# Softmax exponentials per unit on ScalarE with bias and summed output, and sinks in float32, in an attention and mixture-of-experts kernel

## The chip, the cores and the metric

The kernel runs on one core of a Trainium2 chip. The metric is the device time of one execution in microseconds (us). The kernel before has a median of 838.93 us over three runs (838.45 to 840.20). Engines: PE is the matmul engine (TensorE), PEld its weight load, DVE is VectorE, ACT is ScalarE, POOL is GpSimd, SP the engine whose queue issues most DMAs.

## The reference, cut to what matters

```python
# q, k, v: (4, 8, 768, 64) float32; n_sink 4; window 128
scores = (q @ k.transpose(0, 1, 3, 2)) / np.sqrt(64)
keep = (key < 4) | ((query - key >= 0) & (query - key < 128))
scores = np.where(keep, scores, -1e9)
a = np.exp(scores - scores.max(-1, keepdims=True))
a = a / (a.sum(-1, keepdims=True) + 1e-9)
x = (a @ v).transpose(0, 2, 1, 3).reshape(3072, 512)
noisy = x @ w_gate + np.log1p(np.exp(x @ w_noise)) * noise      # (3072, 8)
# two largest experts of each row; their softmax, with 1e-9 in the divisor, as weights
out = sum over these two of weight * (np.maximum(x[rows] @ w1[e], 0) @ w2[e])
```

## The kernel before, in words

**Phase one** (0 to 228 us) is the attention and the choice of experts. It has 48 steps n: 16 pairs of heads g (four batches of four pairs), and for each three blocks jj of 256 queries. A step holds four *units* u: two query tiles of 128, two heads. A query tile looks at two key tiles of 128: after masks, each query has 128 keys of the window, kept at columns modulo 128, and four sinks, so a unit is 128 queries by 132 scores (KW), and a step's tile in `cbuf` is 128 x 528, plus one extra column for each unit that holds 1e-9.

A step goes through these functions. `turn` (PE, L280) transposes two key and two query tiles; `turn_c` (ACT, L286) copies all 512 columns out of PSUM into `kq`; `ksink` (POOL, L290) puts the sinks' keys beside them. `qk` (PE, L307) makes the scores S; `prev` (ACT, L310) copies sinks and the earlier key tile into `cbuf`, `cur` (DVE, L315 or L317) puts the masked current tile over it. `mins` (DVE, L327) takes each unit's maximum, `sub` (POOL, helper `minus` at L192) subtracts it from the 528 columns, `exps` (ACT, L334) exponentiates all four units in one instruction with the scale 1/8, `sums` (DVE, L337) adds up each unit with its 1e-9 column, `sums_i` (DVE, L345) inverts the sums. `ptr` (PE, L365) transposes the window's probabilities into P, `ptr_c` (ACT, L368) copies them to CT, `ptr_m` (POOL, L377, or DVE, L375) makes the masked copy CM. The sinks' probabilities are split in a high and a low part in the PE's reduced 32-bit type (fp32r), by `pcopy` (ACT, L356, or POOL, L354) and `plow` (POOL, L192). `pv` (PE) first transposes them (L382), then multiplies CT by v (L388) and CM by the difference dv of neighbouring value tiles (L391; `dv` is on POOL for one pair in four, else on DVE). `sink_c` (ACT, L395) copies the transposed sinks' probabilities to `ps`, `sinks` (PE, L400) multiplies them by the sinks' values `vr` and adds this into the same PSUM tile X. `pv_c` (ACT, L408), `rows` (PE, L413), `rows_c` (DVE, L416, into `xr`) and a DMA to `x_rows` end the step.

The sinks' values of a batch reach `vr` by a memset on POOL (L241), 16 DMAs on SP's queue (L247), a rounding on ACT (`sink_hi`, L251) and the rest on DVE (`sink_lo`, L256). The choice of experts for a finished batch (lines 546 to 870: projections at L590, operations on 48 columns such as L676 on DVE, spreading of row numbers by four matmuls at L808) is mixed in with the next batches. So are loads of the experts' weights through `st`, whose low parts POOL subtracts (`w<-st,w`, at L192). At the end of phase one gathered rows are transposed (T, L883) and their low part `sqn` made on DVE.

**Phase two** (228 to 837 us) runs the eight experts: H (L999 to L1001), Y (L1028 to L1030), the weighted copy of Y on ACT with a per-row scale (L1037), and a scatter to `out` (L1052).

The order of the work is made by `Plan`, a list scheduler in Python that runs while the program is written: each operation has an engine, a cost, a priority (its step plus an offset from the table `PR`; `_0` for the first two pairs, `_9` for the last two) and the operations that it depends on. On each engine the program has the operations in the order of their planned start. For PE, an operation of another *kind* (shape of stationary tile) than the one before is put back. Rings of buffers bound how far engines run apart: five tiles of `cbuf`, three maxima, four sums, three `pcbuf`, two S, two X, one P and one T in PSUM.

Of the kernel before, what the change touches and what calls it, by code (L numbers as in the profile page):

```python
# [20 lines left out]
PR = dict(dv_pool=1, cm_pool=11, gap=1.5, pc_pool=4, warm=1, cur=11.119, cur1=0.687, cur1_0=44.511, cur1_9=-33.328,  # L21
          cur_0=298.594, cur_9=103.16, dv=-0.483, dv_0=16.276, dv_9=183.829, exps=904.17, exps_0=41.004, exps_9=-4.57,
          ga=1192.414, gt=-84.555, ksink=-94.534, ksink_9=51.556, lg=-15.298, load_qk=-1.606, load_v=-787.643,
          mins=168.634, mins_0=-734.152, mins_9=-446.873, nosink=-377.158, nosink_0=-548.293, nosink_9=-11.556,
          pcopy=43.317, pcopy_0=835.726, pcopy_9=1.286, plow=31.263, plow_0=22.235, plow_9=9.949, prev=-44.255,
          prev_0=3.084, prev_9=-520.412, ptr=290.156, ptr_0=2279.933, ptr_9=-183.508, ptr_c=121.858, ptr_c_0=-0.024,
          ptr_c_9=-10.11, ptr_m=217.241, ptr_m_0=-0.246, ptr_m_9=-22.839, pv=-903.99, pv_0=-10.446, pv_9=-0.801,
          pv_c=2.756, pv_c_0=123.068, pv_c_9=40.062, qk=55.827, qk_0=107.566, qk_9=-45.834, rows=41.788, rows_0=71.983,
          rows_9=-173.605, rows_c=-520.43, rows_c_0=-0.232, rows_c_9=0.725, rt=-379.032, sink_c=-1407.554,
          sink_c_0=45.426, sink_c_9=-0.086, sinks=-132.305, sinks_0=-79.407, sinks_9=-258.405, sub=443.589, sub_0=-14.389,  # L30
          sub_9=-3.573, sums=98.341, sums_0=-6.429, sums_9=-5.607, sums_i=29.922, sums_i_0=-62.833, sums_i_9=-0.83,
          t0=294.759, t2=376.526, tgroup=-1.35, tgroup_0=-158.265, tgroup_9=240.162, tgroup_c=-950.066, tgroup_c_0=76.182,
          tgroup_c_9=-18.757, w1=-543.239, ksink_0=-147.432, stay=3020.27)
# [161 lines left out]
def attention(tc, plan, consts, cst, sh, q, k, v, xbuf):  # L195
# [20 lines left out]
    cbuf = consts.tile([128, plan.rings["C"], 4, KW + 1], F32, name="cbuf")  # L216
    nc.gpsimd.memset(cbuf[:, :, :, KW:], 1e-9)

    pcbuf = consts.tile([128, plan.rings["pc"], 128], F32R, name="pcbuf")
    nc.gpsimd.memset(pcbuf.bitcast(F32), 0.0)  # L220
    bit = [consts.tile([128, 1], dt, name=nm) for nm, dt in (("biti", I32), ("bit", F32))]
    nc.gpsimd.iota(bit[0], pattern=[[0, 1]], base=0, channel_multiplier=1)
    nc.vector.tensor_scalar(bit[0], bit[0], 3, 1, op0=OP.logical_shift_right, op1=OP.bitwise_and)
    nc.vector.tensor_scalar(bit[1], bit[0], -1.0, None, op0=OP.mult)
    bit = bit[1]
    vst = [plan.next("st") for _ in range(sh.B)]
# [16 lines left out]
    def sink_values(b):  # L243
        for u in range(4):
            for x in range(4):
                r = 4 * NS * u + NS * x
                nc.sync.dma_start(vs(b)[r:r + NS, u // 2, :, u % 2, :],  # L247
                                  dram(v, (b * HP * 2 + u % 2) * S * D, [[D, NS], [2 * S * D, HP], [1, D]]))

    def sink_hi(b):  # L250
        nc.scalar.activation(get("vr", b, [128, 2, HP, 2, D], F32R), vs(b), AF.Copy)  # L251

    def sink_lo(b):

        t = get("vr", b)
        nc.vector.scalar_tensor_tensor(t, t.bitcast(F32), bit, vs(b), op0=OP.mult, op1=OP.add)  # L256
# [1048 lines left out]
```

## Time and profile before

| what | before |
|---|---|
| median of three runs | 838.93 us (838.45 to 840.20) |
| the profiled execution's own time | 838.36 us |
| its span, first to last instruction | 836.8 us |
| PE busy | 801.9 us (96%) |
| PEld busy | 682.0 us (82%) |
| DVE busy | 442.0 us (53%) |
| ACT busy | 345.6 us (41%) |
| POOL busy | 437.0 us (52%) |

The profile is one execution with every instruction's start and length. Busy times count instructions in flight; matmuls are pipelined and overlap, so what a matmul costs is read from start to start. The granted clock (PEclk) is a share of PE's full speed. A wait is the idle time of an engine just before an instruction, put down to what released it.

### The profile page before, as it was taken

The page shows a single profiled execution, that of the slowest core. Times are in us where ns is not written, and L with a number is a line of the kernel's source. Part 1 is how long each engine was busy: PE and PEld are TensorE (multiplying, and loading weights), DVE is VectorE, ACT ScalarE, POOL GpSimd, SP SyncE. Part 2 cuts the span into 40 slices and gives each one's busy share as a digit, 9 for nine tenths or more (in the row PEclk, how much of TensorE's full clock was granted, in tenths as well). Part 3 has the DMA queues.
Part 4 walks back from the last instruction along what each step waited for, and adds up shares of the span by engine and source line. Part 5 has one row for each costly group of instructions (what it writes and reads, how often), then busy time and mean ns, then how long its engine had stood idle before and what let it go on. Part 6 is the DMA issues. An engine that isn't in the chain of part 4 may idle for free.

```text
span 836.8 us, 13639 instructions
## 1 busy us (share of the span) xinstructions
PE 801.9 (96%) x4901; PEld 682.0 (82%) x4901; DVE 442.0 (53%) x1098; ACT 345.6 (41%) x685; POOL 437.0 (52%) x602
## 2 busy tenths in 40 slices
PE   6999998998899999999999999999999999999995
PEld 3776776776689989888988988898898889889984
DVE  5788979897573444155345435534543553454210
ACT  4787776775422243234233333413333341333211
POOL 5565866877416742263652746365274636617303
PEclk9999999999999999999999999999999999999998
DMA  6749877754544665165355626535462643544113
GB/s 119 152 90 235 183 184 175 177 137 114 163 115 110 167 149 133 16 160 127 69 100 130 118 40 162 126 68 100 129 118 40 162 126 66 104 119 68 26 23 45
DMA packets 151814, 97.23 MB, mean 116 GB/s; under 512 B 100704, under 2 KB 129376, under 8 KB 151744
## 3 DMA queue, kind: packets, MB, share of 16 engines
q1 hardware_dynamic: 137744, 67.93, 31.6%
q0 software_dynamic: 14000, 28.40, 19.7%
q8 instruction: 39, 0.64, 0.3%
q14 instruction: 31, 0.25, 0.1%
HBM read 67.44 MB, written 28.85 MB: 115 GB/s over the span
## 4 chain that ended last, share of the span: by engine, by line
PE 77%; DVE 8%; issue 5%; POOL 4%; DMA 3%; ACT 2%; SPq 0%; another core or an unknown queue 0%; DVEq 0%; POOLq 0%; ACTq 0%
PE H L999 11%; PE H L1000 11%; PE H L1001 11%; PE Y L1030 10%; PE Y L1028 10%; PE Y L1029 10%; PE S L307 3%; PE X L388 2%; PE T L280 2%; PE P L365 1%; PE Y L1034 1%; PE Y L1033 1%; POOL out L1052 1%; DMA x_rows<-xr 1%; PE X L391 1%
## 5 line engine op out<-in xcount | busy, mean ns | idle before, releaser
L1052 POOL DMA_INDIRECT out<-y,idx x56 | 93.0, 1660 | 238.6 <-ACT y L1037 228.8
L840 POOL DMA_INDIRECT xg<-x_rows,rt_idq x182 | 183.4, 1008 | 55.5 <-issue 51.8
L1017 DVE SCALAR_TENSOR_TENSOR h<-H,h 128x384 fp32r<-128x384 f32 (+1 forms) x192 | 80.8, 445 | 224.7 <-ACT h L1010 224.7
L999 PE MATMUL H<-skn,w 128*128 128x384 f32 (+2 forms) x544 | 187.5, 345 | 0.0
L1010 ACT ACTIVATE h<-H 128x384 fp32r<-128x384 f32 (+2 forms) x136 | 68.0, 500 | 288.0 <-PE H L1001 287.9
L1000 PE MATMUL H<-sqn,w 128*128 128x384 f32 (+2 forms) x544 | 186.7, 343 | 0.0
L1001 PE MATMUL H<-skn,w 128*128 128x384 f32 (+2 forms) x544 | 186.0, 342 | 0.0
L999 PEld LDWEIGHTS H<-skn,w 128*128 128x128 f32 x544 | 102.5, 188 | 8.8 <-issue 0.8
L1000 PEld LDWEIGHTS H<-sqn,w 128*128 128x128 f32 x544 | 102.5, 188 | 7.5
L1001 PEld LDWEIGHTS H<-skn,w 128*128 128x128 f32 x544 | 102.5, 188 | 3.9
L1028 PE MATMUL Y<-w2b,h 128*128 128x512 f32 x196 | 76.8, 392 | 0.9 <-ACT h L1010 0.9
L1030 PE MATMUL Y<-w2b,h 128*128 128x512 f32 x196 | 77.1, 393 | 0.6 <-DVE h L1017 0.6
L1028 PE MATMUL Y<-w2a,h 128*128 128x512 f32 x196 | 77.5, 395 | 0.0
L1029 PE MATMUL Y<-w2a,h 128*128 128x512 f32 x196 | 76.9, 392 | 0.0
L1030 PE MATMUL Y<-w2a,h 128*128 128x512 f32 x196 | 76.9, 392 | 0.0
L1029 PE MATMUL Y<-w2b,h 128*128 128x512 f32 x196 | 76.8, 392 | 0.0
L192 POOL TENSOR_TENSOR cbuf<-cbuf,mn 128x528 f32<-128x528 f32 x48 | 52.1, 1087 | 25.4 <-DVE mn L327 20.2
L307 PE MATMUL S<-kq 64*128 64x264 f32 (+1 forms) x384 | 56.6, 406 | 3.8 <-DVE cbuf L317 2.6
L897 ACT ACTIVATE skn<-xtn 128x512 fp32r<-128x512 f32 (+1 forms) x49 | 28.9, 598 | 58.8 <-DVE xtn L888 58.8
L1030 PEld LDWEIGHTS Y<-w2b,h 128*128 128x128 f32 x196 | 36.8, 188 | 9.1 <-DVE h L1017 1.0
L307 PEld LDWEIGHTS S<-kq 64*128 64x128 f32 x384 | 31.8, 192 | 14.7 <-issue 4.8
L1030 PEld LDWEIGHTS Y<-w2a,h 128*128 128x128 f32 x196 | 36.8, 188 | 8.4
(193 smaller groups left out, 1361.6 us busy)
## 6 DMA issues: line engine op xcount, KB each, us to landing
st<-in_moe_w SPq DMA_DIRECT2D x36, 512.0 KB
st<-in_moe_w SPq DMA_DIRECT2D x112, 128.0 KB
out<-zt SPq DMA_DIRECT2D x31, 256.0 KB
vn<-in_v SPq DMA_DIRECT2D x16, 384.0 KB
x_rows<-xr SPq DMA_DIRECT2D x48, 128.0 KB
kn<-in_k SPq DMA_DIRECT2D x30, 192.0 KB
qn<-in_q SPq DMA_DIRECT2D x30, 192.0 KB
xg<-x_rows,rt_idq POOLq DMA_INDIRECT x182, 2.9
```

The costliest lines, as they stand in the source:

```text
L192: eng.tensor_tensor(out, a, b, op=OP.subtract)
L307: nc.tensor.matmul(p[:, :2 if j else 1], kq(g)[r, j // 2, 2 + j % 2, NS:], x[:, :2 if j else 1], start=True, stop=True)
L840: nc.gpsimd.indirect_dma_start(out=x[:, i, :], out_offset=None, in_=xbuf.rearrange("r (q d) -> (r q) d", d=sh.SW), in_offset=bass.Indirect ...
L999: nc.tensor.matmul(p, w[:, 0, i], xh, start=(i == 0), stop=False)
L1000: nc.tensor.matmul(p, w[:, 0, i], xl, start=False, stop=False)
L1001: nc.tensor.matmul(p, w[:, 1, i], xh, start=False, stop=(i == DC - 1))
L1010: nc.scalar.activation(get("h", FC * q + f, [128, 896], F32R)[:, :width], get("H", FC * q + f), AF.Relu)
L1017: nc.vector.scalar_tensor_tensor(h[:, o:o + s1 - s0], p[:, s0:s1], 0.0, h[:, s0:s1].bitcast(F32), op0=OP.max, op1=OP.subtract)
L1028: nc.tensor.matmul(p, hh, w[:, 0], start=(f == 0), stop=False)
L1029: nc.tensor.matmul(p, hh, w[:, 1], start=False, stop=False)
L1030: nc.tensor.matmul(p, hl, w[:, 0], start=False, stop=(f == FC - 1))
L1052: d = nc.gpsimd.indirect_dma_start(out=out, out_offset=bass.IndirectOffsetOnAxis(ap=c["idx"][:size(e, t), e, t:t + 1], axis=0), in_=get("y ...
```

## The change

- The mask constants change sign, and the scores with them: `turn_c` becomes `turn_k` (ACT, 256 columns of keys, L270) and `turn_q` (DVE, 256 columns of queries, times -1/8, L275). `mins` takes the minimum.
- `sub` is gone. `exp_sum` (ACT, L322) does one unit of 132 columns at a time, with scale -1, the unit's minimum as bias and the unit's sum as second output. `sums` is gone; `sums_a` adds 1e-9 to four sums (30 steps on DVE, L325, and 18 on POOL). The extra columns of `cbuf` go.
- The sinks' probabilities stay float32: `plow` is gone, `pcopy` has 16 columns (36 steps on ACT, L343, 12 on POOL, L341), and their transposition is an operation of its own, `pctr` (L346), ahead of `pv`. `vr` is float32 and filled by four DMAs a batch (L239); both roundings go. The product with the sinks' values (L385) is a float32 matmul.
- `dv` is on POOL for three pairs in four, and the masked copy CM on DVE for 16 of 48 steps (four before).
- All offsets in `PR` are others, and `sinks` has no kind of its own any more.

The numbers of `PR` are left out of the diff.

```diff
+    def turn_k(g, gi, ti):
+        nc.scalar.activation(kq(g)[:, gi, :2, NS:], get("T", ti)[:, :2], AF.Copy)
+
+    def turn_q(eng, g, gi, ti):
+        o, x = kq(g)[:, gi, 2:, NS:], get("T", ti)[:, 2:]
+        if eng == "DVE":
+            nc.vector.tensor_scalar(o, x, -1.0 / math.sqrt(D), None, op0=OP.mult)
+        else:
+            nc.scalar.activation(o, x, AF.Copy, scale=-1.0 / math.sqrt(D))
...
-        nc.vector.tensor_reduce(get("mn", n, [128, 4]), C(n), op=OP.max, axis=AX.X)
-
-    def sub(n, eng):
-        minus(nc.gpsimd if eng == "Pool" else nc.vector, C(n), C(n),
-              get("mn", n)[:, :, None].to_broadcast([128, 4, KW]))
-
-    def exps(n):
-        nc.scalar.activation(C(n), C(n), AF.Exp, scale=1.0 / math.sqrt(D))
-
-    def sums(n):
-        nc.vector.tensor_reduce(get("sm", n, [128, 4]), cbuf[:, n % plan.rings["C"]], op=OP.add, axis=AX.X)
+        nc.vector.tensor_reduce(get("mn", n, [128, 4]), C(n), op=OP.min, axis=AX.X)
+
+    def exp_sum(n, u):
+        c = C(n)[:, u, :]
+        nc.scalar.activation(c, c, AF.Exp, scale=-1.0, bias=get("mn", n)[:, u:u + 1], accum_out=get("sm", n, [128, 4])[:, u:u + 1])
+
+    def sums_a(n, eng):
+        (nc.gpsimd if eng == "Pool" else nc.vector).tensor_scalar(get("sm", n), get("sm", n), 1e-9, None, op0=OP.add)
...
-    def plow(n):
-        t, c = pcs(n, 1)
-        minus(nc.gpsimd, t, c, pcs(n, 0)[0].bitcast(F32))
+    def pctr(n):
+        nc.tensor.transpose(get("X", XA[n], [128, 4, 128], F32, "ps")[:, 2, :], pcs(n), idf)
...
-            nc.tensor.matmul(get("X", XA[n])[:, a, :], get("vr", b)[:, a, i].rearrange("p h d -> p (h d)"), get("ps", n),
+            nc.tensor.matmul(get("X", XA[n])[:, a, :], vs(b)[:, a, i].rearrange("p h d -> p (h d)"), get("ps", n),
                              start=False, stop=True, skip_group_check=True)
...
-            op("Pool", 1.0, z, lambda b=b: sink_zero(b), w=[("st", vst[b])])
-            plan.dma(z, lambda b=b: sink_values(b), .9, r=[("go", 0)], w=[("st", vst[b])], n=16)
-            z += 9 if g else 0
-            op("ACT", .95, z, lambda b=b: sink_hi(b), r=[("st", vst[b])], w=[("vr", b)])
-            op("DVE", 1.2, z, lambda b=b: sink_lo(b), r=[("st", vst[b])], w=[("vr", b)])
+            op("Pool", 1.0, z, lambda b=b: sink_zero(b), w=[("vr", b)])
+            plan.dma(z, lambda b=b: sink_values(b), .25, r=[("go", 0)], w=[("vr", b)], n=4)
...
-            op("Pool", 1.03, n + .4 + P(g, "sub"), lambda n=n: sub(n, "Pool"), r=[("mn", n)], w=[("C", n)])
-            op("ACT", .53, n + .4 + P(g, "exps"), lambda n=n: exps(n), w=[("C", n)])
...
+            for u in range(4):
+                op("ACT", .26, n + .4 + P(g, "exps") + .001 * u, lambda n=n, u=u: exp_sum(n, u), r=[("mn", n)], w=[("C", n)], u=[("sm", n)])
...
-            op("PE", .14, n + .6 + P(g, "sinks"), lambda n=n: sinks(n), r=[("ps", n), ("vr", g // HP)], w=[("X", xa)], kind=3)
+            op("PE", .22, n + .6 + P(g, "sinks"), lambda n=n: sinks(n), r=[("ps", n), ("vr", g // HP), ("X2", xa)], w=[("X", xa)])
```

The change moves instructions on every engine. On ACT, a stretch of steps in the middle of phase one stood so before (L334 is the exponential, L310 `prev`, L395 `sink_c`, L408 `pv_c`; the number behind a name tells buffers' uses apart):

```order
L310 ACTIVATE cbuf_142<-S_742 128x2x132
L310 ACTIVATE cbuf_142<-S_749 128x2x132
L334 ACTIVATE cbuf_142<-cbuf_142 128x4x132
L395 ACTIVATE ps_777<-X_754 128x128
L408 ACTIVATE xtn_784<-X_725 128x256
L310 ACTIVATE cbuf_142<-S_779 128x2x132
L310 ACTIVATE cbuf_142<-S_790 128x2x132
L408 ACTIVATE xtn_784<-X_754 128x256
L334 ACTIVATE cbuf_142<-cbuf_142 128x4x132
```

and a stretch of steady steps now (L322 the exponential of one unit, L301 `prev`, L270 `turn_k`, L380 `sink_c`, L343 `pcopy`, L354 `ptr_c`):

```order
L322 ACTIVATE cbuf_142,sm_741<-cbuf_142,mn_727 128x132
L301 ACTIVATE cbuf_142<-S_732 128x264
L322 ACTIVATE cbuf_142,sm_741<-cbuf_142,mn_727 128x132
L301 ACTIVATE cbuf_142<-S_738 128x264
L322 ACTIVATE cbuf_142,sm_741<-cbuf_142,mn_727 128x132 x2
L270 ACTIVATE kq_670<-T_762 128x2x128
L380 ACTIVATE ps_780<-X_771 128x128
L343 ACTIVATE pcbuf_143<-cbuf_142 128x16
L322 ACTIVATE cbuf_142,sm_789<-cbuf_142,mn_768 128x132 x2
L301 ACTIVATE cbuf_142<-S_782 128x264
L322 ACTIVATE cbuf_142,sm_789<-cbuf_142,mn_768 128x132 x2
L354 ACTIVATE CT_811<-P_752 128x512
```

Four exponentials stand where one stood, with copies that PE's next matmuls read between them.

On PE, the end of a step stood so before (L382 to L391 `pv`, L400 `sinks`, L307 `qk`):

```order
L382 MATMUL X_892<-idr_68,pcbuf_144 128x128
L388 MATMUL X_892<-CT_837,vn_459 64x128 x4
L391 MATMUL X_892<-CM_845,dv_547 64x128 x4
L307 MATMUL S_909<-kq_843 128x264 x2
L307 MATMUL S_920<-kq_843 128x264 x2
L382 MATMUL X_924<-idr_68,pcbuf_144 128x128
L388 MATMUL X_924<-CT_860,vn_702 64x128 x4
L391 MATMUL X_924<-CM_872,dv_794 64x128 x2
L400 MATMUL X_892<-ps_912,vr_368 128x128 x2
```

and now (L346 `pctr`, L264 `turn`, L351 `ptr`, L398 `rows`, L373 and L376 `pv`, L298 `qk`, L385 `sinks`):

```order
L346 MATMUL X_826<-idf_66,pcbuf_143 128x128
L264 MATMUL T_828<-idf_66,kn_634 128x128 x2
L264 MATMUL T_828<-idf_66,qn_665 128x128 x2
L351 MATMUL P_839<-idf_66,cbuf_142 128x128 x4
L398 MATMUL X_771<-idf_66,xtn_833 128x128 x2
L373 MATMUL X_826<-CT_717,vn_558 64x128 x4
L376 MATMUL X_826<-CM_730,dv_638 64x128 x4
L298 MATMUL S_868<-kq_670 128x264 x2
L298 MATMUL S_878<-kq_670 128x264 x2
L385 MATMUL X_826<-ps_837,vr_155 128x128 x2
```

The transposition of the sinks' probabilities stands ahead of `pv` with other transpositions in between, and the sinks' matmuls come behind the next scores, followed by another full-width tile. In phase one PE changes between kinds of tile (full width, scores, `pv`, logits) 209 times before and 174 times now.

On SP's queue, behind the first pair's loads, stood:

```order
L264 DMA kn<-in_k 128x6x64 x2
L268 DMA vn<-in_v 128x12x64 x2
L264 DMA qn<-in_q 128x6x64 x2
L247 DMA st<-in_v 4x4x64 x16
L264 DMA kn<-in_k 128x6x64 x2
L264 DMA qn<-in_q 128x6x64 x2
L247 DMA st<-in_v 4x4x64 x16
```

and now stands:

```order
L248 DMA kn<-in_k 128x6x64 x2
L248 DMA qn<-in_q 128x6x64 x2
L239 DMA vr<-in_v 4x4x64 x4
L248 DMA kn<-in_k 128x6x64 x2
L248 DMA qn<-in_q 128x6x64 x2
L239 DMA vr<-in_v 4x4x64 x4
L252 DMA vn<-in_v 128x12x64 x2
```

The first loads of v (`vn`) moved behind the second and third pairs' keys and queries and behind the sinks' values, of which there are four DMAs instead of 16.

## Rows read from the trace of the kernel before

**Rows 1.** The page's chain of work that ended last, shares of the span by engine.
```profile
PE 77%; DVE 8%; issue 5%; POOL 4%; DMA 3%; ACT 2%; SPq 0%; another core or an unknown queue 0%; DVEq 0%; POOLq 0%; ACTq 0%
```
**Rows 2.** Table of stretches: window and length (us); busy (instructions) by engine, PEclk, DMA share, GB/s.
```profile
228.00:837.00 609.00, 597.30 (x2995) 529.81 (x2995) 257.59 (x609) 192.37 (x307) 285.39 (x303) 0.99 0.46 101
...
140.50:144.00 3.50, 3.29 (x28) 3.04 (x29) 2.94 (x10) 0.69 (x2) 0.81 (x3) 0.57 0.34 112
199.00:202.50 3.50, 3.41 (x26) 2.63 (x27) 1.38 (x4) 0.31 (x2) 1.67 (x4) 0.51 0.00 0
0.00:228.00 228.00, 204.59 (x1907) 152.17 (x1908) 184.45 (x489) 153.26 (x379) 151.63 (x299) 0.97 0.67 156
```
**Rows 3.** PE's waits, 30 to 228 us, five of eleven: us together, times, longest.
```profile
PE X L391 <- POOL CM L377: 2.6, 2, 2.4
PE X L382 <- DVE xr L416: 2.6, 3, 1.4
PE S L307 <- DVE cbuf L317: 2.6, 1, 2.6
PE T L883 <- DVE sqn L192: 1.7, 1, 1.7
PE X L590 <- DVE sqn L192: 1.4, 1, 1.4
...
```
**Rows 4.** Timeline of PE: start and length (us), instruction, count.
```profile
49.80 0.44 PE L400 MATMUL X<-ps,vr 128*128 128x128 f32 x2
50.17 1.16 PE L307 MATMUL S<-kq 64*128 64x264 f32 x8
51.26 0.44 PE L400 MATMUL X<-ps,vr 128*128 128x128 f32 x2
51.54 0.41 PE L413 MATMUL X<-idf,xtn 128*128 128x128 f32 x2
...
61.39 0.60 PE L365 MATMUL P<-idf,cbuf 128*128 128x128 f32 x4
61.83 0.40 PE L413 MATMUL X<-idf,xtn 128*128 128x128 f32 x2
...
255.23 0.99 PE L808 MATMUL X<-rt_idw,y 128*128 128x49 f32 x8
256.04 0.48 PE L1028 MATMUL Y<-w2b,h 128*128 128x512 f32 x1
```
**Rows 5.** Groups by shape: count, busy us, mean ns, idle before and its releasers.
```profile
L192 POOL TENSOR_TENSOR cbuf<-cbuf,mn 128x528 f32<-128x528 f32 x48 | 52.1, 1087 | 25.4 <-DVE mn L327 20.2 <-DVE ri L345 2.5 <-ACT cbuf L310 1.3
...
L337 DVE TENSOR_REDUCE sm<-cbuf 128x4 f32<-128x532 f32 x48 | 33.3, 697 | 6.9 <-ACT cbuf L334 6.2 <-issue 0.4
...
L334 ACT ACTIVATE cbuf<-cbuf 128x528 f32<-128x528 f32 x48 | 31.0, 645 | 7.9 <-POOL cbuf L192 7.5 <-POOL cbuf L320 0.2
...
L368 ACT ACTIVATE CT<-P 128x512 f32<-128x512 f32 x48 | 28.5, 594 | 9.6 <-PE P L365 9.4
...
L416 DVE TENSOR_TENSOR xr<-X,ri 128x256 f32<-128x256 f32 x48 | 19.6, 416 | 6.5 <-ACT cbuf L310 4.0 <-PE X L413 1.2 <-DMA x_rows<-xr 1.1
...
L408 ACT ACTIVATE xtn<-X 128x256 f32<-128x256 f32 x48 | 18.3, 385 | 0.7 <-PE X L400 0.2
L192 POOL TENSOR_TENSOR pcbuf<-cbuf,pcbuf 128x32 fp32r<-128x32 f32 x48 | 15.4, 322 | 10.1 <-ACT pcbuf L356 9.3
...
L1037 ACT ACTIVATE y<-Y,wc 128x512 f32<-128x512 f32 x49 | 32.7, 687 | 20.5 <-issue 9.5 <-PE Y L1030 8.5
```
**Rows 6.** Timeline of ACT near 60 us.
```profile
59.77 0.22 ACT L356 ACTIVATE pcbuf<-cbuf 128x32 fp32r<-128x32 f32 x1
59.89 0.38 ACT L408 ACTIVATE xtn<-X 128x256 f32<-128x256 f32 x1
```
**Rows 7.** Timelines of POOL and of DVE near 137 us.
```profile
136.52 2.37 POOL L192 TENSOR_TENSOR w<-st,w 128x1024 fp32r<-128x1024 f32 x1
...
137.16 1.79 DVE L676 TENSOR_TENSOR rt_no<-lg,rt_ln 128x48 f32<-128x48 f32 x1
```

More of the change, by code (lines that the diff above doesn't have):

```diff
@@ L20 @@
 BIG = 1.0e30
[L21 to L33, printed above, removed]
@@ new lines @@
+PR = dict(q_act=0, pc_act=6, dv_pool=3, cm_pool=8, gap=1.5, warm=1, cur=6.212, cur1=30.949, cur1_0=-144.713,
+          cur1_9=-33.891, cur_0=-12.056, cur_9=-18.958, dv=3.274, dv_0=-278.111, dv_9=342.632, exps=297.122,
+          exps_0=209.134, exps_9=-50.261, ga=93.328, gt=0.65, ksink=-5.567, ksink_9=-276.227, lg=102.464,
+          load_qk=-733.078, load_v=12.682, mins=115.281, mins_0=-31.788, mins_9=420.916, nosink=114.907,
+          nosink_0=-479.411, nosink_9=-7.063, pcopy=43.473, pcopy_0=2.536, pcopy_9=-390.484, plow=-13.038, plow_0=132.694,
+          plow_9=4.672, prev=-1.045, prev_0=-7.487, prev_9=-356.64, ptr=407.425, ptr_0=1729.29, ptr_9=2.505, ptr_c=35.93,
+          ptr_c_0=1.258, ptr_c_9=-1.339, ptr_m=0.047, ptr_m_0=-211.157, ptr_m_9=-50.086, pv=-9.501, pv_0=58.046,
+          pv_9=-2.788, pv_c=87.342, pv_c_0=-460.967, pv_c_9=199.59, qk=187.385, qk_0=1.948, qk_9=-55.352, rows=135.557,
+          rows_0=-6.669, rows_9=-190.627, rows_c=-77.185, rows_c_0=-493.979, rows_c_9=44.215, rt=261.822, sink_c=-3.965,
+          sink_c_0=-215.524, sink_c_9=-15.688, sinks=-17.005, sinks_0=555.169, sinks_9=-52.34, sub=0.741, sub_0=44.605,
+          sub_9=155.711, sums=90.473, sums_0=-2.958, sums_9=19.574, sums_i=198.375, sums_i_0=227.586, sums_i_9=-15.447,
+          t0=17.19, t2=605.816, tgroup=563.483, tgroup_0=497.079, tgroup_9=-619.763, w1=324.979, ksink_0=54.485,
+          stay=2652.466, sums_a_0=-81.209, sums_a_9=667.452, sa_pool=3, turn_q_0=357.013, sums_a=-98.619,
+          turn_k_9=-190.251, turn_q=152.241, pctr=-6.86, pctr_9=-660.598, turn_k=-50.244, pctr_0=456.927,
+          turn_q_9=-135.589, turn_k_0=4.616)
@@ L214, in attention @@
     nc.vector.memset(m0[:, :NS], 0.0)
[L216 to L226, printed above, removed]
+    cbuf = consts.tile([128, plan.rings["C"], 4, KW], F32, name="cbuf")
+    pcbuf = consts.tile([128, plan.rings["pc"], 128], F32, name="pcbuf")
+    nc.gpsimd.memset(pcbuf, 0.0)
     def C(n):
-        return cbuf[:, n % plan.rings["C"], :, :KW]
+        return cbuf[:, n % plan.rings["C"]]
     def vs(b):
-        return get("st", vst[b], [128, 1024], F32, "early").rearrange("p (a g h d) -> p a g h d", a=2, h=2, d=D)
+        return get("vr", b, [128, 2, HP, 2, D])
     def warm():
@@ L244, in sink_values @@
         for u in range(4):
[L245 to L256, printed above, removed]
+            nc.sync.dma_start(vs(b)[NS * u:NS * (u + 1), u // 2, :, u % 2, :],
+                              dram(v, (b * HP * 2 + u % 2) * S * D, [[D, NS], [2 * S * D, HP], [1, D]]))
     def load_qk(nm, g, gi):
@@ L380, in pv @@
     def pv(n):
-        x = get("X", XA[n], [128, 4, 128], F32, "ps")
-        nc.tensor.transpose(x[:, 2, :].bitcast(F32R), pcbuf[:, n % plan.rings["pc"], :], idr)
+        x = get("X", XA[n])
         for m in range(2):
@@ L439, in turns @@
         op("PE", .43, z + P(g, "tgroup"), lambda: turn(g, gi, ti), r=[(nm, g, gi) for nm in nms], w=[("T", ti)], u=[(nm, g) for nm in nms])
-        op("ACT", .49, z + P(g, "tgroup_c"), lambda: turn_c(g, gi, ti), r=[("T", ti)], w=[("kq", g, gi)], u=[("kq", g)])
-        op("Pool", .14, z + P(g, "ksink"), lambda: ksink(g, gi), r=[("kq", g, 0), ("kq", g, gi)], w=[("ks", g, gi)], u=[("kq", g)])
+        op("ACT", .29, z + P(g, "turn_k"), lambda: turn_k(g, gi, ti), r=[("T", ti)], w=[("kt", g, gi)], u=[("kq", g)])
+        e = "ACT" if (g * NJ + gi) % 8 < PR.get("q_act", 0) else "DVE"
+        op(e, .34 if e == "DVE" else .29, z + P(g, "turn_q"), lambda: turn_q(e, g, gi, ti), r=[("T", ti)], w=[("qt", g, gi)], u=[("kq", g)])
+        op("Pool", .14, z + P(g, "ksink"), lambda: ksink(g, gi), r=[("kt", g, 0), ("kt", g, gi)], w=[("ks", g, gi)], u=[("kq", g)])
     def loads_v(g):
```

36 lines of the change are left out of this document (17 added, 19 removed).

## The prediction, made before the changed kernel had run

> **What bounds the kernel now.** I read the chain of waits first. It runs through PE for 77% of the span, then DVE 8% and POOL 4%, and ACT has 2% [rows 1]: what PE issues and what it waits for decides, and ACT is nearly free of blame today. The table of stretches comes next [rows 2]. Phase two (228 to 837 us) has PE busy 597.3 of 609 us, and the change touches none of its lines; it enters only by starting earlier or later. So everything is decided in the first 228 us, where PE is busy 204.6 us. The 23.4 us between are all that removing waits can win there. Two stretches also run at the lower clock: 140.5 to 144 at a granted 0.57 and 199 to 202.5 at 0.51, close to the 1.2 GHz level, where 7.0 us of time hold about 3.8 us of full-speed work, so 3.2 us are lost. Both follow a PE wait of about 2.5 us.
>
> The waits of PE from 30 to 228 us say who owns the idle time [rows 3]: eleven rows, 14.4 us together. 2.6 are for POOL's masked copy CM, 2.6 for the transposed outputs xr of DVE, 2.6 for a cbuf that DVE copies, 3.1 for DVE's sqn at the end of the phase; the other six rows make 3.5. The rest of the 23.4, 9.0 us, lies before 30 us, where the pipeline fills. DVE is late because POOL is: a DVE operation on 48 columns (L676) took 1.79 us, inside a POOL subtraction of 2.37 us (w<-st,w) that began at 136.52 [rows 7].
>
> **PE's own work: +4.5 us.** The sinks' product becomes float32. A float32 matmul stands as two records here: L808 has four matmuls and eight records, at 0.10 us each from start to start [rows 4], with a full 128x128 weight. A 128-column pass with such a weight takes 0.11 (L365, four in 0.44). So two sink matmuls become four records, 4 x 0.11 = 0.44, in place of 0.28 for the pair ahead of L413, where the weight's shape does not change; +0.16 in 48 steps is +7.7. Against it, the order has 174 instead of 209 places where PE changes between kinds of tile in phase one. The same pair of L400 takes 0.37 ahead of L307, so a change costs 0.09: 35 x 0.09 = -3.2. The transpose of the sinks' probabilities stays one record and only moves ahead of pv (0). Bounds: +2, if the second record of each pair were covered, and +9, if no change of tile were saved. By the sum +4.5.
>
> **POOL: 55 us off its queue.** The subtraction goes, 48 x 1.087 = -52.1, and the low part of the sinks' probabilities, 48 x 0.322 = -15.4 [rows 5]. Added are eight subtractions of neighbouring values, which hold 2.5 times the columns of L416, so at least 1 us each (+8 to +12), and 18 tiny additions at under 0.25 (+4). POOL's large operations on the routing and on the weights' low part (such as the 2.37 us of rows 7) stay.
>
> **DVE: 10 us off.** The row sums go, 48 x 0.697 = -33.3, and eight subtractions of values, -8. Scaling q is 48 copies of 256 columns from PSUM, by L416's 0.416 +20.0; twelve more masks of 384 to 512 columns +8; thirty additions of 1e-9 on four columns, a third of L416 or less, +4. What DVE loses by standing behind POOL shrinks with POOL's 55 us.
>
> **ACT: 39 us on.** One exponential of 0.645 becomes four of 132 columns. Between 32 columns (L356, 0.22 us in rows 6) and 528 (0.645) a column costs 0.86 ns, so 132 columns 0.31. A pointer operand shows in the pair L1037 and L368, both 512 columns out of PSUM, as 687 - 594 = 93 ns; so 0.40 each, and 192 x 0.40 - 31.0 = +45.8. Copying keys alone saves 48 x (0.594 - 0.385) = -10.0; twelve more sink copies +2.8. ACT goes from 153.3 to about 192 of 228 us, 84%. PE with its additions has 209, so ACT is second and the time follows PE. The price of one exponential is the unknown here: the trace has no ACT operation with a second output. The low end is 0.20 (start to start of L356, 0.12, plus 100 columns), the high end 0.63, if the sum is fetched by a further instruction as long as L356's 0.22. I take 0.40, the row without a second instruction, since the order shows one instruction for each.
>
> L356 started 0.12 us before the next instruction on ACT though it lasted 0.22 [rows 6], so short ACT operations overlap. Against that stands the Trainium skill, VectorE: DVE Perf Modes, section The TRN2 errata: an SBUF-to-SBUF ScalarE operation pays 224 cycles besides its elements at 1.2 GHz, between instructions, so that many small tiles each pay it, which speaks against cutting one exponential into four. By that page the four would occupy 4 x 0.39 = 1.56 us a step from start to start, against 1.2 by the rows, and phase one would still be PE's; the same rule would give 0.21 for L356's 0.12, so on this row the trace does not agree.
>
> **What the waits do.** The 7.8 us for CM, xr and cbuf come from POOL's queue or from DVE behind it; I count four fifths as gone, -6.2. Of the other 6.6 a quarter, -1.7, because sqn at the end waits for gathers and for routing that the change leaves. The two half-clock stretches follow two of the waits that go: -3.2. In the first 30 us the chain of each of the first steps loses the subtraction (1.09), and the sinks' values lose their two roundings and 12 of 16 DMAs. Against it, SP's queue now has six loads of 192 KB, qn of the second pair and kn and qn of the third, ahead of the first v: 1.15 MB at phase one's mean of 156 GB/s [rows 2] are 7.4 us. PE's order fills most of that: ahead of the first pv stand eight turns, 24 score matmuls and three ptr, where there were three, 12 and two; five turns and one ptr of 0.44 and three times the 1.09 of four score matmuls [rows 4] are 5.9 us of work brought forward. At most 1.5 us of v's lateness is left; three steps of the subtraction are 3.3. I take -2. Together -13 (from -20 to 0).
>
> New: ACT's free time in a step falls from (228 - 153.3)/48 = 1.56 us to 0.75, and behind four exponentials (1.2 us) stand the copies that PE needs: CT, ps, xtn and the scores' own. The order puts other ACT work between the four, and PE has other steps to issue. I let it show in one step of fourteen: +4 (0 to +8).
>
> **Sum.** +4.5 - 13 + 4 = -4.5 against the profiled execution's 838.36, which is 0.57 under the median of 838.93: **834 us**, its own range 830 to 837. Phase two is taken as moved and otherwise the same.
>
> **Rivals.**
> 1. *ACT becomes the bound* (slower). Each exponential costs more than its columns, because the sum is read out by an instruction of its own. From 0.49 us ACT's sum reaches PE's 209, from 0.59 the whole 228. At 0.52 to 0.63 ACT has 215 to 236 us of work; with the 4% that even PE loses over phase one's best stretches, and the waits at both ends, phase one takes about 238: **848** (844 to 856). For it: nothing on ACT is long enough today to show the price. Against: ACT's overlap in rows 6.
> 2. *The waits stay and PE's passes show* (slower). Routing and the weights' low parts still fill POOL in bursts, both stalls of 2.5 us lie in such bursts, and the new order puts others there. Then +4.5 and a little of ACT's: **842** (841 to 844).
> 3. *Nothing moves.* The gains of phase one are waited off by the weights' loads at the start of phase two, or cancel against PE's passes: **839** (837.3 to 840.6).
> 4. *All waits go* (fast). PE's records overlap; the weight loads' busy time, PEld, is 152.2 of 228 us, so there is room for the extra records, and the 13 become 18: **826**. The Trainium skill, Perfetto Trace Analysis, section Identifying the Most-Contended Engine, says that matmul busy time is a poor measure of the distance to the limit and that weight-load busy time is a better one; the row's 67% is in its favour, though rows 4 show PE starting records back to back.
>
> **How the numbers follow.** Forecast 0.40, rival 1 0.21, rival 2 0.15, rival 3 0.17, rival 4 0.07. A measurement of this kernel can tell about 0.2% from no change, 1.7 us, so same is 837.2 to 840.6. Faster: 0.40 + 0.07 = 0.47; same 0.17; slower 0.21 + 0.15 = 0.36. The range 826 to 849 leaves out the upper half of rival 1 and half of rival 4, some 0.14. Most of the chance lies on both sides of zero, so the forecast's own range, 830 to 837, says more of what I believe.
>
> **What would show it.** Right: the four exponentials of a step at 0.3 us from start to start and ACT at 80 to 86% of phase one; sinks at 0.44 a pair; POOL at about 95 us there; no PE wait over 2 us for CM or cbuf; the granted clock at 1.00 from 30 us on; phase two beginning near 223. Wrong by rival 1: PE's waits for ACT (CT, cbuf, xtn) above 10 us in sum and exponentials at 0.5 or more. By rival 2: PE's waits for POOL and DVE still at 10 us or more. By rival 3: phase two begins earlier and ends no earlier.

## The result, and the profile after

The changed kernel takes 841.48 us (median of 19 runs, 840.44 to 843.41), the kernel before 837.68 us beside it (19 runs, 834.97 to 842.47): ratio 1.0039, 95% interval 1.0026 to 1.0052. By the ratio, which goes by the runs' means, it is slower by some 3.3 us (3.8 between the medians), where 4.5 us faster was forecast; the time lies in the range, the sign is wrong. The profiled execution took 843.41 us, the longest of the 19; its span is 841.8 us. Of the runs below, e7 was profiled in an execution of 1326.75 us at a granted clock of 0.56, so only the times of its other twelve executions are used.

The chain of waits of the changed kernel answers to [rows 1]; ACT went from 2% to 6%, POOL from 4% to 2%:

```profile
PE 76%; DVE 8%; ACT 6%; issue 5%; DMA 2%; POOL 2%; SPq 1%; another core or an unknown queue 0%; DVEq 0%; POOLq 0%; ACTq 0%
```

Its table of stretches, with the columns of [rows 2]:

```profile
0.00:234.20 234.20, 213.33 (x2003) 160.66 (x2003) 173.65 (x517) 182.61 (x722) 92.99 (x203) 0.99 0.65 150
...
160.00:165.00 5.00, 3.14 (x22) 2.81 (x23) 2.83 (x8) 2.57 (x11) 0.79 (x6) 0.69 0.85 223
```

POOL fell from 151.6 to 93.0 us and ACT rose from 153.3 to 182.6, but 228 us no longer hold phase one. Its end is the first matmul of H, here in the timeline of PE of the kernel before and then of the changed one:

```profile
227.79 0.69 PE L999 MATMUL H<-skn,w 128*128 128x384 f32 x1
```
```profile
234.19 0.44 PE L984 MATMUL H<-skn,w 128*128 128x384 f32 x1
```

From there to PE's end it is 600 us before and 598 after: the whole loss lies in phase one, and the begin of phase two measures it. Two further profiles of the changed kernel (e11 and e16 below) have 232.4 and 234.1. Up to that begin PE was busy 204.4 us and idle 23.4 before; in the three profiles of the changed kernel it was busy 211.4 to 213.3 and idle 20.9 to 22.2. So PE does not idle longer than before: it is busy 7 to 9 us longer, and only 1 to 2.5 us of idle time went in return.

PE's waits from 30 to 228 us in the changed kernel, against [rows 3]:

```profile
PE X L398 <- ACT xtn L393: 2.9, 4, 1.2
PE X L373 <- ACT ps L380: 2.6, 4, 2.0
PE X L346 <- DVE xr L401: 2.2, 5, 0.7
...
```

All rows from 30 us to the begin of phase two make 12.8 us, where [rows 3] made 14.4. PE's own waits for CM are gone, 0.2 us are left of those for cbuf, and those for xr stay. In their place stand waits for ACT: the copies of X and of the sinks' probabilities. The longest, 2.0 us for `ps`, ends at 161.9; PE is busy 0.14 of the 2 us from 160 to 162, and from 162 to 164 the granted clock is 0.50, the 1.2 GHz level (the row at 160 above). This one is put down to ACT, but ACT itself was idle for DVE's masked copy CM, which stood behind a subtraction of 2.25 us on DVE, side by side with one of POOL's on the weights (156.98 to 159.34). It is the kind of stall that [rows 7] show, and e11, e16 and e2 below have it too (PE waits 2.0, 2.0 and 1.6 us):

```profile
161.04 0.60 ACT L354 ACTIVATE CT<-P 128x512 f32<-128x512 f32 x1 [1.74 <-DVE CM L361]
```
```profile
157.77 2.25 DVE L194 TENSOR_TENSOR dv<-vn 128x640 f32<-128x640 f32 x1
```

The load that the exponentials put on ACT's own queue is seen in its timeline (L322 the exponential of one unit):

```profile
93.34 0.39 ACT L322 ACTIVATE cbuf<-cbuf,mn 128x132 f32<-128x132 f32 x1
93.63 0.19 ACT L322 ACTIVATION_READ_ACCUMULATOR cbuf<-cbuf,mn 128x1 f32 x1
93.72 0.39 ACT L322 ACTIVATE cbuf<-cbuf,mn 128x132 f32<-128x132 f32 x1
```

Every exponential is followed by a second instruction that reads the accumulator. From start to start the exponential takes 0.30 us and the read 0.09, so four units take 1.55 us where one exponential of 528 columns took 0.54 (the median of L334 in the trace before; the expectations below say 0.53). One case shows what follows from it: PE ends a step's X (L385) at 28.2 us, but ACT has begun four exponentials at 28.02 and reaches the copy of X only at 29.84, behind them and one other copy:

```profile
30.26 0.44 PE L398 MATMUL X<-idf,xtn 128*128 128x128 f32 x2 [1.21 <-ACT xtn L393]
```

The groups by shape of the changed kernel, up to 234 us, against [rows 5]:

```profile
L322 ACT ACTIVATE cbuf<-cbuf,mn 128x132 f32<-128x132 f32 x192 | 76.6, 403 | 11.3 <-DVE mn L318 9.9 <-POOL kq L281 0.6 <-DVE rt_tv L735 0.5
...
L322 ACT ACTIVATION_READ_ACCUMULATOR cbuf<-cbuf,mn 128x1 f32 x192 | 38.0, 198 | 0.0
```

And the float32 sinks in PE's timeline, against [rows 4]: a pair (L385, four records) takes 0.45 us ahead of a tile of the same width, where two records took 0.28.

```profile
230.84 0.61 PE L385 MATMUL X<-ps,vr 128*128 128x128 f32 x4
231.29 0.60 PE L868 MATMUL T<-idf,xg 128*128 128x128 f32 x4
```

### The profile page after: what moved, and what is told of

Its sections match the earlier page's. It is cut to its first block, busy times and chain, and to the rows that moved or that the text cites. A ratio compares the mean times of both kernels' runs of the same rounds, so it can differ in the third digit from the quotient of the medians.

```text
span 841.8 us, 14009 instructions
## 1 busy us (share of the span) xinstructions
PE 810.1 (96%) x4997; PEld 689.7 (82%) x4997; DVE 431.3 (51%) x1126; ACT 375.4 (45%) x1029; POOL 379.4 (45%) x506
## 4 chain that ended last, share of the span: by engine, by line
PE 76%; DVE 8%; ACT 6%; issue 5%; DMA 2%; POOL 2%; SPq 1%; another core or an unknown queue 0%; DVEq 0%; POOLq 0%; ACTq 0%
PE H L984 11%; PE H L985 10%; PE H L986 10%; PE Y L1015 10%; PE Y L1013 9%; PE Y L1014 9%; PE S L298 3%; ACT cbuf L322 3%; PE X L373 2%; PE X L385 2%; PE T L264 2%; PE X L376 1%; PE Y L1019 1%; PE Y L1018 1%; DVE mn L318 1%
## 5 line engine op out<-in xcount | busy, mean ns | idle before, releaser
L322 ACT ACTIVATE cbuf<-cbuf,mn 128x132 f32<-128x132 f32 x192 | 76.6, 403 | 11.3 <-DVE mn L318 9.9
L298 PE MATMUL S<-kq 64*128 64x264 f32 (+1 forms) x384 | 56.7, 412 | 1.5 <-POOL kq L281 1.0
L298 PEld LDWEIGHTS S<-kq 64*128 64x128 f32 x384 | 33.0, 195 | 14.2 <-issue 5.6
```

Of the source, the lines that this page charges most:

```text
L298: nc.tensor.matmul(p[:, :2 if j else 1], kq(g)[r, j // 2, 2 + j % 2, NS:], x[:, :2 if j else 1], start=True, stop=True)
L322: nc.scalar.activation(c, c, AF.Exp, scale=-1.0, bias=get("mn", n)[:, u:u + 1], accum_out=get("sm", n, [128, 4])[:, u:u + 1])
```

## The experiments

Theory A: ACT paces phase one; the exponentials with their second outputs load it so much that PE waits for ACT's copies. Theory P: the loss is PE's own float32 passes. The runs went to four chips. On one of them (e1 to e4, e9 to e11) the kernel before takes about 839 us, on the other three 856. The extra time lies in phase two: from its begin to PE's end the changed kernel takes 597.8 us in e11 and 613.5 in e16, and the runs as a whole 598 to 602 on the first chip and 608 to 616 on the others. So a run is read by its ratio to the kernel before on the same chip, and by the begin of phase two. That begin comes from one execution each, and the three profiles of the changed kernel differ by 1.8 us in it. The kernel before was profiled on one chip alone; its 19 executions spread over 7.5 us.

| run | ratio (95% interval) | phase two begins (us) | ACT busy, 0 to 228 us |
|---|---|---|---|
| before | 1 | 227.8 | 153.3 |
| changed | 1.0039 (1.0026 to 1.0052) | 234.2 | 180.1 |
| e11, changed again | 1.0033 (1.0014 to 1.0053) | 232.4 | 180.5 |
| e16, changed again | 1.0030 (1.0010 to 1.0050) | 234.1 | 179.4 |
| e1, sinks reduced | 1.0036 (1.0017 to 1.0056) | 230.5 | 183.1 |
| e2, one exponential | 0.9908 (0.9878 to 0.9937) | 222.0 | 146.4 |
| e5, no second output | 0.9956 (0.9930 to 0.9981) | 227.6 | 168.4 |
| e7, planner's cost | 1.0013 (0.9994 to 1.0033) | | |
| e8, one bias, order remade | 1.0063 (1.0042 to 1.0084) | 235.5 | 146.8 |
| e12, one bias, order kept | 0.9955 (0.9939 to 0.9970) | 227.5 | 147.8 |
| e13, queries on ACT | 1.0053 (1.0034 to 1.0072) | 233.5 | 191.4 |
| e15, extra ACT copies | 1.0095 (1.0066 to 1.0124) | 242.9 | 186.7 |
| e3, before, sinks float32 | 1.0026 (1.0006 to 1.0047) | 231.5 | 154.8 |
| e4, before, four exponentials | 1.0240 (1.0210 to 1.0271) | 249.2 | 180.8 |
| e6, before, no subtraction | 0.9874 (0.9843 to 0.9906) | 218.3 | 156.0 |
| e9, before, one bias | 0.9895 (0.9857 to 0.9933) | 217.9 | 158.7 |
| e10, before, exponentials' half | 1.0142 (1.0104 to 1.0181) | 237.7 | 189.3 |
| e14, as e10, sinks float32 | 1.0171 (1.0147 to 1.0194) | 243.8 | 185.2 |

**The two theories, from both kernels.** e1 takes the float32 passes out of the changed kernel; it leaves out the low part of the sinks' product:

```diff
...
-        nc.scalar.activation(get("ps", n, [128, 128]), get("X", XA[n])[:, 2, :], AF.Copy)
+        n % 12 or nc.scalar.activation(get("vh", n // 12, [128, 2, HP, 2, D], F32R), vs(n // 12), AF.Copy); nc.scalar.activation(get("ps", n, [128, 128], F32R), get("X", XA[n])[:, 2, :], AF.Copy)
...
-            nc.tensor.matmul(get("X", XA[n])[:, a, :], vs(b)[:, a, i].rearrange("p h d -> p (h d)"), get("ps", n),
+            nc.tensor.matmul(get("X", XA[n])[:, a, :], get("vh", b)[:, a, i].rearrange("p h d -> p (h d)"), get("ps", n),
```

> The changed kernel with the sinks' product alone in the reduced 32-bit type again, in one pass and without the split into high and low parts (the low part of the sinks' product is left out); the order on PE, DVE and POOL is the same, ACT has four more roundings of the sinks' values. Theory P (PE's own passes are the loss): the pair of sink matmuls goes from 0.45 to 0.28 us, 48 x 0.17 = 8.2 us less, so about 833.5 us where the changed kernel has 841.5, ratio to before 0.995. Theory A (ACT paces phase one): the saved passes turn into longer waits of PE for ACT, 3 us less at most, ratio about 1.001.

Ratio 1.0036, as the changed kernel. PE's waits of this run from 30 us on:

```profile
PE X L373 <- ACT ps L380: 5.8, 9, 2.5
PE X L398 <- ACT xtn L393: 4.7, 9, 1.5
```

PE was busy 200.4 us in the first 228 instead of 207.2 to 208.5, and waited 10.5 us for these two copies instead of 5.5. Up to the begin of phase two it was busy 10 to 12 us less than in the changed kernel and idle 7 to 8 more. Theory P falls as the cause: within the interval of 0.2% nothing is won, the saved passes became waits.

e2 takes ACT's load off instead; it leaves out the bias and puts a constant for the sum:

```diff
-        nc.scalar.activation(c, c, AF.Exp, scale=-1.0, bias=get("mn", n)[:, u:u + 1], accum_out=get("sm", n, [128, 4])[:, u:u + 1])
+        if u == 0:
+            nc.scalar.activation(C(n), C(n), AF.Exp, scale=-1.0)
...
```

> The changed kernel with one exponential of 528 columns per step without bias and without the second output; the maximum is not subtracted and a constant stands for the sum. The order of all the rest is the same. ACT is relieved of 48 x (1.55 - 0.53) = 49 us. Theory A: PE's waits for ACT (xtn, ps, kq: about 7 us) and the later starts behind them go, so 833 to 835 us, ratio about 0.996. Theory P: ACT is not what PE waits for in the end, at most 2 us less, ratio 1.002 to 1.004.

Ratio 0.9908, and phase two begins 10 to 12 us earlier: theory A, by more than it asked. PE's waits for ACT, e2's stretch and its exponential:

```profile
PE X L373 <- ACT ps L380: 1.8, 2, 1.6
...
PE X L398 <- ACT xtn L393: 1.2, 2, 0.8
```
```profile
0.00:228.00 228.00, 212.80 (x2040) 163.33 (x2041) 174.53 (x521) 146.40 (x390) 91.06 (x203) 1.00 0.70 159
```
```profile
L322 ACT ACTIVATE cbuf<-cbuf 128x528 f32<-128x528 f32 x48 | 30.8, 642 | 11.6 <-DVE mn L318 9.2 <-DVE vm L722 1.1 <-DVE ri L333 0.4
```

Up to the begin of phase two, PE of e2 is busy 206.8 us and idle 15.2, with the same matmuls. So of the changed kernel's loss against e2, 6 to 7 us are idle time and 5 to 7 are longer busy time, in which the half-clock stretches account for an estimated 1.7 to 3.4 (the busy time at the lower clock, times the missing share of the clock); e2 has none. The exponential of e2 still stands behind DVE's minimum (9.2 us), as the four of the changed kernel do (9.9). That wait is not what e2 saved.

The same two causes were put into the kernel before, e3 and then e4:

```diff
-            nc.tensor.matmul(get("X", XA[n])[:, a, :], get("vr", b)[:, a, i].rearrange("p h d -> p (h d)"), get("ps", n),
+            nc.tensor.matmul(get("X", XA[n])[:, a, :], get("vr", b)[:, a, i].rearrange("p h d -> p (h d)").bitcast(F32), get("ps", n).bitcast(F32),
```
```diff
...
-        nc.scalar.activation(C(n), C(n), AF.Exp, scale=1.0 / math.sqrt(D))
+        for u in range(4):
+            c = C(n)[:, u, :]
+            nc.scalar.activation(c, c, AF.Exp, scale=1.0 / math.sqrt(D), bias=zero, accum_out=scrap[:, u:u + 1])
```

> The kernel before with nothing but the sinks' product as a float32 matmul (same data, same order on every engine). Theory P: 96 matmuls become 192 records, +0.17 us for each of 48 pairs, +8 us, ratio 1.010. Theory A (the waits of phase one are longer than PE's work, so added passes hide in them): +3 us or less, ratio up to 1.004.

> The kernel before with its exponential cut into four of 132 columns, each with a bias operand (zero) and a second output that nobody reads; subtraction, sums and order stay. ACT gets 48 x (1.55 - 0.53) = +49 us, from 153 to 202 of 228. Theory A: PE's waits for ACT grow by 6 us or more, ratio 1.007 or above. Theory P: ACT has room for it, within 2 us, ratio 0.998 to 1.002.

e3 is slower by 0.26% (0.06 to 0.47), 2.2 us of the 8.2 us of added passes; the rest hides in waits. e4 is slower by 2.4%, 20 us, in an order that was not made for it. Its waits of PE from 30 to 245 us:

```profile
PE X L405 <- ACT ps L400: 6.4, 10, 1.1
PE P L370 <- ACT CT L373: 4.4, 5, 1.7
```

**What of the exponentials it is.** e5 keeps the four with their bias and drops `accum_out`; `sums_a` writes the constant.

```diff
-        nc.scalar.activation(c, c, AF.Exp, scale=-1.0, bias=get("mn", n)[:, u:u + 1], accum_out=get("sm", n, [128, 4])[:, u:u + 1])
+        nc.scalar.activation(c, c, AF.Exp, scale=-1.0, bias=get("mn", n)[:, u:u + 1])
...
```

> The changed kernel with its four exponentials per step and their bias, but without the second output; a constant stands for the sum. Order as in the changed kernel. ACT loses 192 reads of the accumulator at 0.092 us from start to start, 17.7 of the 49 us that one exponential per step took off. Theory A (time goes with ACT's load): about a third of that run's 10 us, 3 to 4 us less than the changed kernel, 838 us. Rival (the cut into four is what makes a step's chain longer, the reads stand beside it): 1.5 us less at most. Rival (the second output alone is the loss): 8 us less or more, 833 us.

0.83% below the changed kernel, about 7 us: between the third that theory A gave and the rival of the second output alone. The 192 reads are 17.7 us of ACT's 49 and bring some 7 of e2's 11 us, 0.4 us for each microsecond; the other 31 us bring 4. That the last microseconds on ACT cost most is suggested by this, not shown: the two runs are from different chips and their intervals are wide.

**Whether the gain was there at all.** e6 empties `sub` in the kernel before:

```diff
-        minus(nc.gpsimd if eng == "Pool" else nc.vector, C(n), C(n),
-              get("mn", n)[:, :, None].to_broadcast([128, 4, KW]))
+        return
```

> The kernel before without the subtraction of the maximum on POOL (the maximum is still taken, and not used); the same order on every engine. POOL loses 48 x 1.09 = 52 us. The step of the prediction that waits fall by 13 us with POOL's queue: 8 us less or more, ratio 0.990 or below. Rival (POOL has room, the waits come from the routing's bursts): 3 us less at most, ratio 0.996 or above.

Ratio 0.9874, phase two 9.5 us earlier: the step on POOL's queue was right in the order before. e10 then puts the first half of the change into that order (besides the lines shown, the maximum is taken negated, `turn_c` carries the scale, `sub` and `sums` return at once, the 1e-9 is left out), and e14 adds the sinks in float32 without a low part (`plow` returns at once, pcbuf and ps are float32).

```diff
...
-        nc.scalar.activation(C(n), C(n), AF.Exp, scale=1.0 / math.sqrt(D))
+        [nc.scalar.activation(C(n)[:, u, :], C(n)[:, u, :], AF.Exp, bias=get("mn", n)[:, u:u + 1],
+                              accum_out=get("sm", n, [128, 4])[:, u:u + 1]) for u in range(4)]
...
```

> The kernel before, in its own order, with the first half of the change alone: four exponentials per step with the unit's negated maximum as bias and the unit's sum as second output, no subtraction, no sums on DVE (the 1e-9 is left out); the sinks stay split and in the reduced type. POOL loses 52 us, DVE 33, ACT gains 49. Theory A (ACT's 49 us cost more than POOL's 52 and DVE's 33 bring): slower than the kernel before, ratio 1.003 to 1.012. Rival (the loss of the changed kernel lies in the sinks' float32 passes or in its new order): ratio 0.995 or below.

> The run with the first half of the change in the order of the kernel before, and besides the sinks' probabilities in float32 without their low part (48 operations of 0.32 us on POOL go, the sinks' product is a float32 matmul, their values stay split). ACT's load is as in that run. Theory A: within 0.4% of that run's 1.0142, 1.010 to 1.018, so the rest of what brings the changed kernel to 1.0036 is ACT's and DVE's relief and its order. Rival (the sinks in float32 are themselves a gain of 1%): 1.002 to 1.008.

The exponentials' half alone is slower by 1.4%, more than the 0.3 to 1.2% expected, though POOL lost its subtraction and DVE its sums; from e6 to e10 phase two moves from 218.3 to 237.7. The float32 sinks do not win it back (1.0171). So the step from 1.017 to 1.004 lies in the rest of the change: the queries' copies on DVE, which take 10 us off ACT, the new order, and the loads, `dv` and CM that moved with it. e13 below, on the same chip as e14, has the queries' copies on ACT in the new order and reads 1.0053: most of the step, some 1.2%, is the new order and what moved with it, not the queries. How much of that is the order alone was not tried. It softens ACT's price too: the four exponentials cost 20 us in the order before (e4) and 11 in the new one (e2).

**Order or load.** e7 gives the scheduler another cost for an exponential:

```diff
-                op("ACT", .26, n + .4 + P(g, "exps") + .001 * u,
+                op("ACT", .387, n + .4 + P(g, "exps") + .001 * u,
```

> The changed kernel with 0.387 us, the measured spacing of one exponential with its read, in place of 0.26 as the cost in the list scheduler; every instruction stays, only their order moves. Theory O (ACT's load is fine, the order made for a too short exponential is what makes PE wait): 4 us less or more. Theory A (the load itself): within 3 us of the changed kernel either way.

1.0013, some 2 us under the changed kernel, with overlapping intervals: the order made with too short an exponential costs little against this one. Other orders were not tried here. e13 puts the queries' scaled copies on ACT:

```diff
-            nc.vector.tensor_scalar(o, x, -1.0 / math.sqrt(D), None, op0=OP.mult)
+            nc.scalar.activation(o, x, AF.Copy, scale=-1.0 / math.sqrt(D))
```

> The changed kernel with the scaled copies of the queries on ACT instead of DVE at the same places of the program: ACT gets 48 x 0.26 = 12.7 us more, DVE loses 20. Theory A (each us of ACT's load costs 0.2 to 0.4 us, as 49 us gave 10 and 17.7 us gave 7): ratio 1.007 to 1.011. Rival (ACT's harm is in the exponentials' place in the chain of a step, not in its load): 1.001 to 1.005, as the changed kernel.

1.0053 lies just above the range of the rival and under that of theory A, and decides nothing, since DVE lost 20 us at once. e15 loads ACT alone:

```diff
...
-        nc.scalar.activation(xt(n), get("X", XA[n])[:, :2, :], AF.Copy)
+        nc.scalar.activation(xt(n), get("X", XA[n])[:, :2, :], AF.Copy); nc.scalar.activation(scrap, ge[:, None, :].to_broadcast([128, 2, 128]), AF.Copy)
```

> The changed kernel with 48 more copies of 256 columns on ACT that nobody reads, each behind a step's copy of X (pv_c); no other engine gains or loses anything and the order is the same. ACT gets about 48 x 0.26 = 12.5 us. If ACT's load as such sets the time: as for the exponentials, 0.2 to 0.4 us each, ratio 1.007 to 1.010. If the exponentials cost by their place between a step's minimum and its transposition, and ACT has room elsewhere: 1.003 to 1.006, and the queries' copies of the run before hid nothing behind DVE's relief.

> The changed kernel itself beside the run with the extra copies, on the same chip. All theories: 1.002 to 1.006.

1.0095 against 1.0030 for the changed kernel on the same chip, and phase two 8.8 us later. In the groups of e15 the copy is

```profile
L393 ACT ACTIVATE scrap<-ge 128x256 f32<-128x256 f32 x48 | 19.9, 414 | 0.0
```

with 0.31 us from start to start, 14.7 us in all. By the ratios (0.65% of 856 us) each microsecond put on ACT costs 0.4 us (0.2 to 0.6 by the intervals), though no other instruction reads what these copies write. The begin of phase two gives 0.6, but e15's profiled execution is the longest of its six, 867.44 us against a median of 864.56. So time on ACT's queue costs by itself, at a price that fits the 0.4 of e5's reads. That e13 cost little would then mean that DVE's 20 us were worth most of ACT's 12.7, which was not tried alone. The control e11 (on the first chip) confirms the changed kernel:

> The changed kernel itself, beside the two others on the same chip. All theories: ratio to the kernel before near the 1.0039 measured, 1.001 to 1.007, with phase two beginning 4 to 7 us later than before.

**A version that beats both.** A softmax row allows any constant (but for the 1e-9 in the divisor), so the four units of a step, which lie side by side in a row of `cbuf`, can share one bias for each row, and one exponential does. e8 puts this into the changed kernel, e12 too, but with the scheduler's costs left alone so that the order stays, both without the 1e-9; e9 puts it into the kernel before, with `sub` returning at once and the scale in `turn_c`. The lines are e9's:

```diff
...
-        nc.vector.tensor_reduce(get("mn", n, [128, 4]), C(n), op=OP.max, axis=AX.X)
+        nc.vector.tensor_reduce(get("mn", n, [128, 1]), C(n), op=OP.max, axis=AX.XY, negate=True)
...
-        nc.scalar.activation(C(n), C(n), AF.Exp, scale=1.0 / math.sqrt(D))
+        nc.scalar.activation(C(n), C(n), AF.Exp, bias=get("mn", n))
```

> The changed kernel with one minimum per query over the step's four units as bias, so that one exponential of 528 columns does; the sums are a reduction on DVE again and the 1e-9 is left out. ACT loses 48 x (1.55 - 0.63) = 44 us, DVE gets 33 us and loses 10. Theory A: 831 to 835 us, faster than the kernel before by 4 to 7 us. Rival (DVE, now at about 195 of 228 us, takes ACT's place): 839 us or more.

> As the run with one bias per step, but the list scheduler keeps the costs of the changed kernel, so that the order of everything is the changed kernel's; the sums (reductions on DVE, 48 x 0.70 = 33 us) stand where the additions of 1e-9 stood. Rival (DVE's added load made that run slow): ratio 1.003 or above, as there. Theory O2 (the order that the scheduler made for other costs made it slow, DVE's load did not): near the run with one exponential and no sums, ratio 0.992 to 0.997.

> The kernel before, in its own order, with the largest score of a query over the step's four units as bias of its one exponential (the maximum is taken negated, and the copy of the transposed keys and queries carries the scale), so the subtraction on POOL goes; sums on DVE, sinks split as before. ACT gets 0.093 for each of 48 pointers, 4.5 us. Theory A: the gain of the run without the subtraction stays (ratio 0.9874 there): 0.986 to 0.992, phase two begins near 219. Rival (the wait of the exponential for the maximum, with nothing of POOL between, costs on ACT's queue what the subtraction cost): 0.996 or above.

e8 was slow (1.0063) where 831 to 835 us were expected. Its rival was DVE's load, but e12 has the same DVE work in the kept order and 0.9955. The stretches of e8 and then of e12:

```profile
0.00:228.00 228.00, 208.88 (x1959) 156.11 (x1960) 185.88 (x529) 146.77 (x380) 85.60 (x184) 0.99 0.66 152
```
```profile
0.00:228.00 228.00, 208.41 (x2005) 158.71 (x2006) 190.34 (x535) 147.82 (x387) 87.27 (x185) 1.00 0.67 154
```

The remade order was the cost, some 1.1%, with phase two 8 us later at nearly the same work on every engine. e9 is the fastest complete kernel: 830.01 us beside 839.73 for the kernel before, ratio 0.9895. Its exponential has 528 columns and a pointer:

```profile
L334 ACT ACTIVATE cbuf<-cbuf,mn 128x528 f32<-128x528 f32 x48 | 35.1, 733 | 0.0
```

POOL is nearly as empty as in the changed kernel (98.0 us in the first 228, where that has 92.3), at 4 us (48 x 0.09) on ACT in place of 49. A unit whose largest score lies far under that of the other three would lose range in its sum, which the bias per unit would not.

## Why the prediction was wrong, by its own steps

- **PE's own work, +4.5.** The size of the passes was right: 0.45 in place of 0.28 for a pair, forecast 0.44. But the time does not feel them whole: e3 shows 2.2 us of 8.2, e1 nothing beyond the noise. A sum of PE's work holds only where PE waits for nothing. The -3.2 for fewer changes of tile was not measured by itself.
- **POOL's queue and the waits, -13.** Right in kind for the waits: e6 shows 10.6 us (1.26%) for the subtraction alone, and the waits for CM and cbuf are gone from the changed kernel, while those for xr stayed. The -3.2 for the half-clock stretches in it failed: 1.00 from 30 us on was forecast, but in all three profiles of the changed kernel a stretch at 0.50 to 0.53 follows PE's 2.0 us wait near 160 us, at whose root DVE stands behind its `dv` beside a POOL subtraction, as in the stalls that were to go. In all, PE's waits from 30 us on fell from 14.4 to 12.8 us.
- **ACT, +4 (0 to +8): the failed step.** The prediction took 0.40 for an exponential, "the row without a second instruction, since the order shows one instruction for each", and 1.2 us for four from start to start. The order's one row becomes two instructions in the trace, and four take 1.55, so the term left out 0.35 x 48 = 17 us on ACT's queue. e2 against the changed kernel puts the price of the four exponentials at 10 to 12 us where +4 was forecast, and e5 says where the difference lies: without the reads the kernel measures 0.9956, near the 0.9948 (834 against 838.36) that the forecast stands for, and 4 us above e2, the size of the term. Dropping the reads alone turns the sign back. That the forecast's total fits e5 so well is in part luck, since the passes came out 2 us cheaper and POOL's relief 2 us smaller than forecast.
- **"ACT is second and the time follows PE".** As a rule this failed too: ACT was busy 182.6 of 234.2 us, 78%, less than the 84% forecast, and each further microsecond on it cost 0.4 us (e15). ACT's copies feed PE in the order of one queue, so they come later by what stands before them (the 1.2 us wait at 30.26 us is one case); in e1 PE waits longer for two of them as soon as it has less work (10.5 us, 2.5 of which are the stall near 160 us). The wait of the exponentials for DVE's minimum does not explain the price, since e2 has it as well.
- **The rivals.** Rival 1 named the mechanism, a read of the sum by its own instruction, with too high a price: 848. Read lengths overlap, so 0.403 + 0.198 us of recorded length take only 0.39 of the queue. Rival 2's 842 is the measured time, and PE's busy time did grow by more than its idle time fell; but its reason was waits for POOL and DVE, and by its own sign, 10 us or more of them, it fails: they make 6.5 us, 8.5 with the one near 160 us that is put down to ACT, and e1 wins nothing by dropping the passes. The gain of 10.6 (e6), ACT's price of 10 to 12 (e2) and 2.2 for the passes (e3) add up to 2 to 4 us slower, near the 3.3 measured; they are from two different orders, so this sum is rough.
- **The rule on short ScalarE operations.** The spacing of one exponential, 0.30 us, is what the rows gave. By the Trainium skill, VectorE: DVE Perf Modes, section The TRN2 errata, the prediction put it at an estimated 0.39, with the pointer's 93 ns of the rows. That agrees with the recorded length of 0.403 but not with the spacing, and the 1.56 us for four met the measured 1.55 only because the reads made up the difference.
- **Phase two, moved and otherwise the same.** Right: 598 us against 600. But it begins at 232 to 234, where 223 was forecast.

## What to carry to other kernels

The second output of an exponential on ACT was a second instruction here: look for it in a trace and count it, at its spacing, before a pass on an idle engine is traded for it. An engine that feeds the bound engine through one in-order queue was no free cover at 78% busy; test the price by adding a copy that nobody reads. Where a bias forces one large operation into several, look for a coarser constant that keeps it whole.
